# Turning queries and keys by DMA instead of on TensorE, in an attention and FFT-gate kernel

## The chip, the cores and the metric

The kernel runs on one core of a Trainium2 chip. The metric is the device time of one execution in microseconds (us), less is better. Most executions of one kernel agree within some tenths of a per cent; a run that is more than 1.5% above the fastest of its kernel is called slow and is left out of the ratios.

## The reference

Four batches of local and global attention feed a gated convolution. Cut to what matters:

```python
# attention: q, k, v are (4 batches, 8 heads, 768 rows, 64)
scores = scale * np.matmul(q, k.transpose(0, 1, 3, 2))
is_global = pos[None, :] < 8                   # the first 8 keys are seen by all queries
is_local = (rel >= 0) & (rel < 96)             # and each query sees its last 96 keys
...                                            # slope bias, mask, softmax
attn = np.matmul(a, v)
# gate
proj = x @ w_proj                              # 512 -> 3 x 512
y = x1 * irfft(rfft(x2) * rfft(filter)) * x3
out = y @ w_out
```

The kernel's score matmuls read queries and keys with the head dimension on the partitions, so both are needed turned (`QT`, `KT`), while they are loaded row by row (`qn`, `kn`). The kernel works on 7 key tiles a batch. A tile has 128 places: the first 8 are for the global keys, the other 120 are for rows of the sequence. So each key tile needs the 8 global key columns in front of its own.

## The kernel before

The kernel is written as a list of operations. Each one names its engine, an expected duration, and keys for what it reads and writes. A list scheduler lays these on the engines' time lines, with a table of small tuned numbers ("nudges") that shift its choices. The program is then emitted in one order, and semaphores are derived from overlapping addresses in that emitted order.

```python
    def load_rows(self, what, dst, src, b, t):           # places 8.. of a tile; 0 to 7 stay
        lo, hi = self.K0[t], self.K0[t] + KL
        self.load("G", dst[P - (hi - lo):P, t, :, 0:self.D], ...)

    def transposes(self, what, t, src, cols):
        b = g.bank()
        def turn(_):
            for i in range(4):
                nc.tensor.transpose(b.f16()[:, P * i:P * i + P],
                                    src[:, 2 * i:2 * i + 2, :], self.ident)
        g.op("P", pe(*[128] * 4), turn, acq=[b], r=["ident", (what + "n", t)] + ..., name=what)
        lo = NG if what == "k" else 0                    # NG = 8: leaves the global columns out
        dst = self.QT[:, :, cols:cols + P] if what == "q" else self.KT[:, :, cols + lo:cols + P]
        g.op("AV", ..., lambda e: self.copy(e, dst, b.f16()...[:, :, lo:]), use=[b],
            w=[(what.upper() + "T", t)], name=what + "T")
        if what == "k" and t == 0:                       # global columns of all 7 tiles
            kv = self.KT.rearrange("p i (t c) -> p i t c", t=7)
            g.op("V", dve(224), lambda _: self.copy(
                "V", kv[:, :, :, 0:NG], kv[:, :, 0:1, NG:2 * NG].to_broadcast([P, 4, 7, NG])),
                r=[("KT", 0)], w=["KTg"])

    def attention(self, b):
        for c in range(3):                               # thirds of a batch
            for t in ([0, 1, 2], [3, 4], [5])[c]:
                self.transposes("q", t, self.qn[:, t], P * t)
            for t in self.GRP[c]:
                self.transposes("k", t, self.kn[:, t], P * t)
            for i in range(4):
                self.scores(i, c, ...)                   # read ("QT", t), ("KT", t) and "KTg"
            ...                                          # values, projection, gate

    def program(out):                                    # the order of emission
        for o in out:
            need[o] = set(o.preds)                       # from keys and PSUM banks alone
            ...
        while len(order) < len(out):
            for e in "AVSGP":                            # first engine whose next op is ready
                if line[e] and need[line[e][-1]] <= done:
                    ...
                    break
```

"A", "V", "S", "G" and "P" are ScalarE, VectorE, SyncE (a DMA queue), GpSimd and TensorE. The small copy (`"KTg"`) reads tile 0's first turned rows and writes 8 columns of every key tile.

## Time and profile before

| | before |
|---|---|
| time, median of 3 runs | 176.94 us (176.42 to 177.24) |
| TensorE busy, of a 175.5 us span | 166.9 us, 95% |
| VectorE, ScalarE busy | 157.0 us, 152.6 us |
| TensorE transposes of `qn`, `kn` tiles | 156 matmuls |
| hardware DMA queue | 4,424 packets, 7.30 MB |

The prediction below reads the page of this kernel. Here are three of its lines that it does not show: the busy tenths of TensorE and VectorE and the granted TensorE clock, in 40 slices of 4.4 us (9 is 90% or more).

```profile
PE   7799999999899799999999999999999999999991
DVE  6669778999999769999999998999899999998960
PEclk9999999999999999999999999999999999999998
```

### The profile page before, as it was taken

To read this page: it belongs to the slowest core of one execution; us is meant where nothing else is said; L and a number is where in the kernel's file an instruction comes from. 1 tells how busy PE (TensorE), PEld (TensorE's weight loads), DVE (VectorE), ACT (ScalarE), POOL (GpSimd) and SP (SyncE) were. 2 spreads that over 40 slices of the span, in tenths; PEclk is the share of its full clock that TensorE was granted. 3 is DMA by queue.
4 is the path that set the end of the run, shared out by engine and by line. 5 is a ranking of instruction groups with operands and counts; after the bars stand their busy time and mean duration, and the time that the engine had idled before them with its cause. 6 is when DMAs were issued, how large, how long until landed. Compare 5 with 4: busy or idle time off the path is not lost.

```text
span 175.5 us, 4566 instructions
## 1 busy us (share of the span) xinstructions
PE 166.9 (95%) x1768; PEld 104.3 (59%) x1768; DVE 157.0 (89%) x368; ACT 152.6 (87%) x304; POOL 75.3 (43%) x97
## 2 busy tenths in 40 slices
PE   7799999999899799999999999999999999999991
PEld 2357777665457567575446669754556674547540
DVE  6669778999999769999999998999899999998960
ACT  8879989999999778999997977999799897968751
POOL 7999986298997699998040300000000000000000
PEclk9999999999999999999999999999999999999998
DMA  5999999999999999999999900000710000043145
GB/s 177 148 145 134 146 200 209 166 152 138 135 166 159 132 141 142 146 144 149 66 63 344 70 4 4 0 0 0 294 70 4 0 2 4 0 159 140 60 166 197
DMA packets 79853, 20.06 MB, mean 114 GB/s; under 512 B 70528, under 2 KB 76888, under 8 KB 79832
## 3 DMA queue, kind: packets, MB, share of 16 engines
q0 software_dynamic: 75408, 12.47, 107.2%
q1 hardware_dynamic: 4424, 7.30, 11.5%
q8 instruction: 14, 0.23, 0.5%
q14 instruction: 7, 0.06, 0.1%
HBM read 25.69 MB, written 6.29 MB: 182 GB/s over the span
## 4 chain that ended last, share of the span: by engine, by line
PE 64%; DVE 14%; DMA 9%; POOL 5%; ACT 5%; issue 2%; ACTq 0%; POOLq 0%; DVEq 0%
PE bank L1098 19%; PE bank L1215 12%; DMA qn<-in_q_dram 9%; PE bank L1159 6%; PE bank L1181 4%; PE bank L1015 4%; PE bank L924 4%; PE bank L938 3%; PE bank L1020 3%; PE bank L975 3%; PE bank L1060 3%; ACT E L990 3%; POOL kn L583 2%; POOL vn L583 2%; PE bank L630 2%
## 5 line engine op out<-in xcount | busy, mean ns | idle before, releaser
L1098 PE MATMUL bank<-xT,w 128*128 128x384 f16 x256 | 45.6, 326 | 0.0
L990 ACT ACTIVATE E<-bank 128x864 f16<-128x864 f32 x48 | 41.0, 923 | 1.7 <-PE bank L975 1.3
L1098 PEld LDWEIGHTS <-w 128*128 128x128 f16 x256 | 23.9, 98 | 15.8 <-issue 0.8
L583 POOL DMA_DIRECT2D kn<-in_k_dram x24 | 21.6, 908 | 14.0 <-PE bank L938 6.6
L583 POOL DMA_DIRECT2D vn<-in_v_dram x29 | 26.2, 922 | 2.0 <-DMA w<-in_moe_w_proj_dram 1.6
L1215 PE MATMUL bank<-wo,y 128*128 128x512 f16 (+1 forms) x100 | 21.8, 371 | 0.1
L583 POOL DMA_DIRECT2D qn<-in_q_dram x21 | 18.6, 892 | 5.9 <-PE bank L755 3.2
L997 DVE TENSOR_TENSOR E<-E,mask 128x864 f16<-128x864 f16 x36 | 20.9, 597 | 0.1
L1039 DVE TENSOR_TENSOR xn<-bank,rc 128x512 f16<-128x512 f32 (+1 forms) x24 | 18.5, 775 | 0.4
L571 ACT ACTIVATE ot<-bank 128x512 f32<-128x512 f32 (+1 forms) x23 | 13.1, 606 | 5.1 <-PE bank L1215 5.0
L1108 ACT CAST g<-bank 128x384 f16<-128x384 f32 x32 | 15.7, 494 | 1.4 <-PE bank L1098 1.2
L1015 PEld LDWEIGHTS <-E 128*128 128x128 f16 x224 | 14.1, 97 | 3.6 <-DVE E L997 1.1
L571 ACT ACTIVATE ab<-bank 128x512 f16<-128x512 f32 x23 | 14.3, 633 | 2.2 <-PE bank L1159 2.0
L1215 PEld LDWEIGHTS <-y 128*128 128x128 f16 x100 | 9.5, 98 | 10.7 <-DVE y L1257 0.8
L1015 PE MATMUL bank<-vn,E 128*128 128x65 f16 x224 | 15.8, 194 | 0.0
L571 ACT ACTIVATE x<-bank 128x384 f16<-128x384 f32 x28 | 13.8, 507 | 2.3 <-PE bank L1098 1.8
L1020 PE MATMUL bank<-vn,E 128*128 128x65 f16 x192 | 15.4, 193 | 0.0
L975 PE MATMUL bank<-QT,KT 64*128 64x216 f16 (+2 forms) x224 | 15.0, 241 | 0.1
L1020 PEld LDWEIGHTS <-E 128*128 128x128 f16 x192 | 13.3, 97 | 0.4
L567 ACT CAST X<-bank 128x512 f16<-128x512 f32 x21 | 12.3, 643 | 0.0
L975 PEld LDWEIGHTS <-KT 64*128 64x128 f16 x224 | 8.3, 94 | 5.6 <-issue 3.0
L924 PE MATMUL bank<-ab,fwd 128*128 128x512 f16 x40 | 11.4, 379 | 0.0
(144 smaller groups left out, 358.2 us busy)
## 6 DMA issues: line engine op xcount, KB each, us to landing
out_dram<-ot SPq DMA_DIRECT2D x23, 256.0 KB
vn<-in_v_dram POOLq DMA_DIRECT2D x28, 120.0 KB, 6.1
kn<-in_k_dram POOLq DMA_DIRECT2D x21, 120.0 KB, 6.0
qn<-in_q_dram POOLq DMA_DIRECT2D x18, 128.0 KB, 6.7
w<-in_moe_w_proj_dram POOLq DMA_DIRECT2D x4, 256.0 KB, 7.3
g<-in_moe_filter_fft_dram POOLq DMA_DIRECT2D x1, 768.0 KB, 12.5
qn<-in_q_dram POOLq DMA_DIRECT2D x3, 192.0 KB, 5.0
kn<-in_k_dram POOLq DMA_DIRECT2D x3, 192.0 KB, 5.1
```

What stands on the lines that cost most here:

```text
L571: self.nc.scalar.mul(out, in_, c)
L583: return self.g.op(eng, 0.57 + 0.00035 * nbytes[0] if eng == "G" else 0.5, lambda _: e.dma_start(dst, src), w=w, r=r, nbytes=nbytes, name= ...
L924: self.nc.tensor.matmul(b.f32(), self.fwd[:, f], src(i, t), start=(n == 0), stop=(n == len(terms) - 1))
L975: nc.tensor.matmul(bs[hh].f32()[:, off:off + w], self.KT[hs, hp, P * m:P * m + P], self.QT[hs, hp, KL * m:KL * m + w], start=(off == 0 and ...
L990: g.op("A", act(864), lambda _: nc.scalar.activation(eo, bs[0].two()[:, :, 0:432].rearrange("p h (m w) -> p h m w", m=2), Act.Exp, scale=s ...
L997: g.op("V", dve(864, 2), lambda _: nc.vector.tensor_mul(eo, eo, mk), r=[("E", hp, gi), ("mask", hp)], w=[("E", hp, gi)], name="masked")
L1015: nc.tensor.matmul(o[:, n, hh], ef[:, at:at + P], vt[:, t, 2 * hp + hh, :], start=first, stop=(t == 0), skip_group_check=True)
L1020: nc.tensor.matmul(o[:, n, hh], ef[:, at:at + P], vt[:, t - 1, 2 * hp + hh, :], start=False, stop=True, skip_group_check=True)
L1039: nc.vector.tensor_mul(to, o[:, :, :, 0:D], rc.to_broadcast([P, 2, 2 * nt, D]))
L1098: nc.tensor.matmul(bk.f32()[:, 0:h], self.w[:, c, o + P * j:o + P * j + P], self.xT[:, c, h * s:h * s + h], start=(c == 0), stop=(c == 3))
L1108: g.op("A", act(h), lambda _: nc.scalar.copy(x3, pts[1].f32()[:, 0:h]), use=[pts[1]], w=[ko], name="x3")
L1215: nc.tensor.matmul(bk.f32()[:, 0:n], y[:, c, P * t:P * t + P], self.wo[:, c, cs], start=(c == 0), stop=(c == 3))
```

## The change

Its intent: 18 of the tiles (all 13 of batch 3; queries 4 and 5 and keys 4 to 6 of batch 2) are turned by the transposing DMA, straight from `qn`/`kn` into `QT`/`KT`. That takes 72 transposes off TensorE and 18 copies off ScalarE and VectorE. The schedule allows 1.9 us of SyncE for each. In batch 3, where even key tile 0 goes that way, two small DMAs put the global rows in front of each `kn` tile, so the transposition itself delivers the global columns, and the small copy falls away. In batch 2 tile 0 is still turned on TensorE, and the small copy stays. The rest of the diff is a new order, a few more idle matmuls (matmuls on dummy data that fill waits of TensorE) and a new expected size of one load in the schedule. All nudges are replaced (cut here).

```diff
-    FAVOUR = 0.1
+    FAVOUR = 0.0
...
-                gap = o.start - at - 2.2 * (at < BEGIN + 1.0)
+                gap = o.start - at - 1.7 * (at < BEGIN + 1.0)
...
+    CROSS = frozenset((b, w, t) for b in (2, 3) for w in "qk" for t in range(7) if b > 2 or t > 3)
...
+    def turned(self, b, what, t, src, cols):
+        if (b, what, t) not in self.CROSS:
+            self.transposes(what, t, src, cols)
+            return
+        dst = (self.QT if what == "q" else self.KT)[:, :, cols:cols + P]
+        keys = [("kng", min(t // 2, 1))] if what == "k" else []
+        self.g.op("S", 1.9, lambda _: self.nc.sync.dma_start_transpose(
+            out=dst, in_=src.rearrange("p h d -> p (h d)")), r=[(what + "n", t)] + keys,
+            w=[(what.upper() + "T", t)], nbytes=(512, 1000), name=what + "T")
+        if what == "k" and t == 0:
+            self.g.writer["KTg"] = self.g.writer[("KT", 0)]
...
-                    self.transposes("q", t, self.qn[:, t], P * t)
+                    self.turned(b, "q", t, self.qn[:, t], P * t)
...
-                    self.transposes("k", t, self.kn[:, t], P * t)
+                    self.turned(b, "k", t, self.kn[:, t], P * t)
...
+                if t == 0 and (b, "k", 0) in self.CROSS:
+                    self.load_global(self.kn, ("kng",), ("kn", 0))
```

## The prediction

> **What bounds the kernel now.** I read the page first, for the share of each engine and for the chain of work that ended last.
>
> ```profile
> PE 166.9 (95%) x1768; PEld 104.3 (59%) x1768; DVE 157.0 (89%) x368; ACT 152.6 (87%) x304; POOL 75.3 (43%) x97
> ...
> PE 64%; DVE 14%; DMA 9%; POOL 5%; ACT 5%; issue 2%; ACTq 0%; POOLq 0%; DVEq 0%
> ```
>
> TensorE is the fullest engine and holds most of the chain, but VectorE and ScalarE are close behind, so an average does not say what a saving on TensorE is worth. Next I asked for the busy time by stage. The columns are start and end, length, then busy time and instructions of PE, PEld, DVE, ACT, POOL, then the granted clock, the DMA share and GB/s.
>
> ```profile
> 0.00:58.00 58.00, 54.03 (x684) 34.43 (x684) 50.08 (x142) 53.55 (x115) 48.28 (x67) 1.00 2.05 159
> 58.00:88.00 30.00, 29.20 (x293) 18.29 (x294) 27.33 (x59) 27.04 (x52) 23.60 (x27) 1.00 2.17 130
> 88.00:102.00 14.00, 13.95 (x142) 8.44 (x142) 13.81 (x29) 12.79 (x25) 3.44 (x4) 1.00 0.88 150
> 102.00:171.00 69.00, 69.00 (x647) 42.74 (x645) 65.32 (x141) 58.37 (x115) 0.00 (x0) 1.00 0.15 57
> 171.00:175.50 4.50, 0.72 (x7) 0.39 (x4) 0.42 (x1) 0.80 (x2) 0.00 (x0) 0.84 0.54 201
> ```
>
> From 88 to 171 us TensorE has no hole at all. A busy PE may still be stalled in small ways, so I counted the columns that its matmuls stream in each stage and divided by 2,400 columns a microsecond (53 ns for 128 columns, against 55 ns from start to start in the chain; two row or column tiles that run together count once). That gives 26.6 us of pure streaming in the 30 us from 58 to 88, but about 81.5 in the 83 us from 88 to 171. So the last 83 us are set by the amount of TensorE work; before that, waits for DMA (one of 9.4 us in the chain, from 49 to 58 us) and VectorE (nearly every piece of the chain from 66 to 88 us) count too.
>
> Then I looked for the transposes that the change removes in the chain in order of time (start, length, what):
>
> ```profile
> 107.22 0.45 PE bank L938 x8
> ...
> 109.61 1.12 PE bank L938 x20
> 110.73 0.34 PE bank L1060 x6
> 111.06 0.89 PE bank L938 x16
> ```
>
> L938 is the TensorE transpose of queries and keys. Batch 3's stand in the chain itself, 4 matmuls in 0.22 us.
>
> **What the Trainium skill says.** "VectorE: DVE Perf Modes", section "The three transpose paths", gives 390 ns for a 128x128 transpose on TensorE and 1309 ns by the DMA crossbar. The trace agrees for TensorE only in kind: one is 219 ns long here, and pipelined ones cost 55 ns each. "Advanced Engine Details and Errata", section "X-Bar Transpose (TRN2)", says that transposing DMAs are as fast as ordinary ones, and "DMA: Bandwidth & Descriptors", section "Latency and other measured facts", has 261 GB/s measured for one kernel. No run here shows either yet. The latter page, section "Issuing engines are not separate DMA queues", says that all queues share the same 16 engines; the trace has both queues at work, and while loads run the engines are full.
>
> **The change, part by part.** A tile is 128 rows of 512 fp16 numbers. The set has 5 tiles of batch 2 (queries 4 and 5, keys 4 to 6) and all 13 of batch 3: 18.
>
> Removed: 18 x 4 = 72 TensorE transposes and 18 copies out of PSUM.
>
> ```profile
> L938 PE MATMUL bank<-ident,kn x84: 216/219/219, 38.1 to 111.7; 128*128 128x128 f16 x84
> ...
> L567 ACT COPY KT<-bank 128x480 f16<-128x480 f16 x15 | 8.8, 604 | 0.6 <-PE bank L938 0.6
> L567 ACT COPY QT<-bank 128x512 f16<-128x512 f16 x13 | 8.0, 626 | 0.5 <-PE bank L938 0.5
> ...
> L567 DVE COPY QT<-bank 128x512 f16<-128x512 f16 x5 | 2.1, 418 | 0.9 <-PE bank L938 0.9
> ```
>
> On TensorE that is 72 x 55 ns = 4.0 us. By their order 17 of the 18 tiles are turned between 87 and 112 us, in the full stretch, so 3.7 us are on the path. The copies: the instruction order of the changed kernel has 10 fewer KT and 6 fewer QT copies of this size on ScalarE (10 x 0.604 + 6 x 0.626 = 9.8 us) and 2 fewer on VectorE (0.8 us). The scheduler then shifts other work to ScalarE: 4 eo copies, one group of xn scalings, and others back. Summing the counts that differ by the durations of these rows, VectorE has some 5 us less and ScalarE some 6 us less. So all three engines lose 3 to 4% together and none becomes the new bound.
>
> Added: 18 transposing DMAs and 2 small ones (the global rows of keys for batch 3) on the SP queue, which until now issues 35 DMAs and waits most of the time:
>
> ```profile
> SPq L1221 <- ACT ot L571: 81.7, 18, 28.5
> ```
>
> At 261 GB/s a tile of 128 KB is 0.5 us of transfer (an estimate, from the skill); the schedule takes 1.9 us of SP and some 1.5 us of DMA for each. At 2 us a tile, 18 are 36 us of the SP queue. Batch 3's queries and keys leave GpSimd from 68 to 98 us and its scores begin at 117 us, so 13 x 2 = 26 us fit between. The DMA engines:
>
> ```profile
> DMA  5999999999999999999999900000710000043145
> GB/s 177 148 145 134 146 200 209 166 152 138 135 166 159 132 141 142 146 144 149 66 63 344 70 4 4 0 0 0 294 70 4 0 2 4 0 159 140 60 166 197
> ```
>
> Each slice is 4.4 us. They are full until slice 23 (101 us) and then nearly idle. The five tiles of batch 2 and the first of batch 3 compete with loads, the rest does not. I put a delay of the loads at up to 2 us, at a place where they are 10 to 20 us ahead.
>
> Moved: the whole order is laid anew (new nudges, and FAVOUR 0 in place of 0.1, so VectorE is not avoided). 25 idle matmuls in place of 16: 14 in front instead of 11, four in a hole before the first values, the rest in small holes. The front ones fill the 1.02 us that PE waits at 6.1 us for the first queries; they remove no wait, and the clock is already 1.00 there, so I give them 0 (plus or minus 0.3).
>
> Sum: -3.7 in the full stretch; -0.3 to -1 for the relieved VectorE before 88 us; +0.3 to +1.5 for what a new order and dependence on DMA landings cost. Net about -3.7, so 176.94 becomes 173.2.
>
> **Rivals.** A: the crossbar is slow. At 1309 ns for each 128x128 block (the skill), a tile is 5.2 us and 18 are 94 us, not before about 160 us for the last. Scores of batch 3 would wait, and the time would be 185 or more. For it: the only figure for this very operation. Against: the same skill's "as fast as regular DMAs", and a schedule with 2 us, which looks measured. At 3 us a tile, batch 3's last third would come some microseconds late: 175 to 178.
>
> B: the SP queue becomes the wait. It takes its DMAs in order, and the stores of batch 1 now stand between transposes that wait for loads. There are six output buffers; a late store holds ScalarE's copy, then a bank, then TensorE. The new order shows such waits on DMA at several ot copies. It would eat 1 to 3 us: 174 to 176.
>
> C: the saving is given back in the first half. If loads and VectorE set when batch 2 and 3 can begin, less TensorE work only makes holes before 112 us. Against it: the streaming count of 81.5 in 83 us. It would leave 175 to 176.
>
> D: a better packing of the first 88 us, where about 7 us of stall lie between 40 and 88, would give 171.
>
> **Range and chances.** The saving by count puts the time at 173.2, just past the 2% line (173.4). D, at 0.2, pulls below 172; B and C, together 0.3, pull to 174 to 176; A in a mild form, 0.07, goes above 176.5, seldom far. Range 170.9 to 176.3. Faster 0.52, same 0.42, slower 0.06.
>
> **What would show each step.** L938 must have 84 matmuls instead of 156, PE busy less by about 4 us net of 9 more idle matmuls (2 us); KT and QT copies of this size on ScalarE, 16.8 us before, must be about 7. From about 88 us to the last matmul TensorE must still be full, and the stretch shorter by 3 to 4 us; if it has holes that end with a DMA into QT or KT, A is true, and the SP queue's timeline will show more than 2 us a tile. Holes that end with ScalarE's ot, itself after a DMA to the output, mean B. A stretch that starts later than 88 us by as much as it is shorter means C. One thing besides time: for batch 2 nothing loads rows 0 to 7 of the key tiles that the crossbar turns, and it writes these rows over the global key columns, so a small numerical error is possible. The prediction is wrong if time falls although PE's last stretch does not shrink, or if DMA landings enter the chain after 88 us.

## More of the kernel before

TensorE is nearly full throughout, and its granted clock is at 9 tenths or more in all but the last slice. The stage from 60 to 80 us (columns: start and end, length, busy time and instructions of PE, PEld, DVE, ACT, POOL, granted clock, DMA share, GB/s) and, in VectorE's timeline (start, length, what), the copy of batch 2's global columns:

```profile
60.00:80.00 20.00, 19.84 (x212) 13.20 (x210) 18.25 (x39) 18.27 (x39) 20.00 (x23) 1.00 2.25 141
```

```profile
61.88 0.26 DVE L567 COPY KT<-KT 128x224 f16<-128x224 f16 x1
```

That copy costs a quarter of a microsecond and stands behind no wait. It is 4 x 7 x 8 = 224 elements a partition: the 8 columns of all seven tiles.

## The result, and the profile after

The change made the kernel slower: 186.68 us median of 4 runs (184.29 to 188.91), against 177.01 us (176.42 to 177.24) for the kernel before. Two of the four runs count as slow; the fast ones are 184.29 and 185.78. The ratio of fast runs is 1.0459, 95% interval 1.0375 to 1.0543. Here and below a ratio is the mean time of one kernel's fast runs over that of the other's fast runs of the same rounds, so it is not quite the ratio of the medians quoted. The result of the changed kernel is correct.

The profile below is of a run of 187.57 us, one of the slow ones. What is read from it does not depend on that: an experiment below (one tile moved) has the same wait at the same place in a fast run.

First the page: busy time, and the share of each engine in the chain that ended last.

```profile
PE 166.1 (89%) x1705; PEld 102.3 (55%) x1705; DVE 149.6 (80%) x359; ACT 149.3 (80%) x301; POOL 75.2 (40%) x97
...
PE 62%; DMA 15%; POOL 8%; DVE 7%; ACT 2%; issue 2%; SPq 1%; POOLq 0%; DVEq 0%; ACTq 0%
```

Work has fallen on every compute engine, VectorE by 7.4 us, TensorE by only 0.8. So more work on them is not the cause. DMA's share of the chain rose from 9% to 15%. The slices (4.6 us each) show where:

```profile
PE   7995999999999960079999999999999999999992
...
DVE  6635669999998820089999998979999999999960
...
PEclk9999699999999996559999999999999999999999
```

TensorE and VectorE both have one long hole, from 66 or 68 to 79 us, and the clock falls there. (It also falls at 19 to 23 us in this slow run; the fast profiles of e1 and e5 do not have that dip, so nothing is read from it.) In the two stages around the hole TensorE is busy 8.07 of 20 us, then 19.89, and the clock is 0.77, then 0.89:

```profile
60.00:80.00 20.00, 8.07 (x116) 5.57 (x115) 6.05 (x14) 8.41 (x16) 11.20 (x13) 0.77 2.36 133
80.00:100.00 20.00, 19.89 (x155) 11.89 (x155) 19.46 (x44) 16.91 (x33) 17.15 (x19) 0.89 1.90 119
```

Who waited for whom is in the list of waits (engine and line, what ended the wait; us in all, times, longest):

```profile
DVE KT L564 <- DMA KT<-kn: 13.3, 1, 13.3
...
PE bank L934 <- DVE xT L564: 11.9, 1, 11.9
ACT QT L564 <- PE bank L934: 11.8, 1, 11.8
POOL qn L580 <- PE bank L934: 9.6, 1, 9.6
```

Read from the top, it is a row of dominoes: each line waits for the one above it. VectorE waits for a DMA, TensorE for VectorE, ScalarE and GpSimd for TensorE. Only the first is a cause. VectorE's timeline there:

```profile
65.30 0.68 DVE L570 TENSOR_SCALAR h<-bank 128x512 f16<-128x512 f32 x1
79.30 0.22 DVE L564 COPY KT<-KT 128x224 f16<-128x224 f16 x1 [13.32 <-DMA KT<-kn]
79.44 0.45 DVE L564 COPY xT<-bank 128x576 f16<-128x576 f16 x1
```

It is the small copy of the global columns, the one that ran at 61.88 us without a wait before. It now waits 13.3 us for the transposing DMA of `kn` into `KT`. Behind it stands the copy of `xT`, which frees the PSUM bank for which TensorE waits. The chain in order of time shows what the DMA did:

```profile
65.84 6.32 DMA kn<-in_k_dram
...
74.85 4.33 DMA KT<-kn
...
79.30 0.22 DVE KT L564
```

The load of a later key tile lands at 72.2 us. Then SyncE issues three transposes, one after another, and the last lands at 79.2 us. In the built program their order is tile 5, tile 6, tile 4 (columns 640, 768 and 512 of `KT`); that matters for e5 below. So a copy that needs tile 0 alone waits until tiles 4, 5 and 6 have been loaded and turned.

Why it waits is in the instruction lists of the two programs, which give the semaphores that each VectorE instruction waits for:

```
before  147 L567 TensorCopy KT<-KT 128x28x8  [waits DVE_49,PE_49]
after   150 L564 TensorCopy KT<-KT 128x28x8  [waits DMAHW3_49,DMAHW4_49,DMAHW2_49,DVE_49]
```

Three DMA semaphores stand there, one for each of keys 4 to 6 of batch 2. The TensorE path wrote a key tile from column 8 on (`lo = NG`). The transposing DMA writes all 128 columns, the 8 global ones included. The keys of the schedule do not know this: `("KT", 4)` and `"KTg"` are different names. In the emitted order the three DMAs come ahead of the copy, so the step that works by addresses has to make the copy wait for them. It is right to do so: the copy has to overwrite what the DMA put there.

### The profile page after: what moved, and what is told of

The parts are those of the page before. It is cut to its first block, busy times and chain, and to the rows that moved or that the text cites. A ratio compares the mean times of both kernels' runs of the same rounds, so it can differ in the third digit from the quotient of the medians.

```text
span 185.8 us, 4477 instructions
## 1 busy us (share of the span) xinstructions
PE 166.1 (89%) x1705; PEld 102.3 (55%) x1705; DVE 149.6 (80%) x359; ACT 149.3 (80%) x301; POOL 75.2 (40%) x97
## 3 DMA queue, kind: packets, MB, share of 16 engines
q1 hardware_dynamic: 14288, 9.72, 21.1%
## 4 chain that ended last, share of the span: by engine, by line
PE 62%; DMA 15%; POOL 8%; DVE 7%; ACT 2%; issue 2%; SPq 1%; POOLq 0%; DVEq 0%; ACTq 0%
PE bank L1106 19%; PE bank L1223 11%; PE bank L1167 10%; DMA qn<-in_q_dram 5%; PE bank L1189 5%; DMA vn<-in_v_dram 4%; PE bank L983 4%; PE bank L920 4%; DMA kn<-in_k_dram 3%; POOL kn L580 2%; DMA KT<-kn 2%; POOL qn L580 2%; PE bank L1068 2%; PE bank L1023 2%; PE bank L1028 2%
## 5 line engine op out<-in xcount | busy, mean ns | idle before, releaser
L1106 PE MATMUL bank<-xT,w 128*128 128x384 f16 x256 | 46.5, 332 | 0.1
L998 ACT ACTIVATE E<-bank 128x864 f16<-128x864 f32 x48 | 41.5, 921 | 2.9 <-PE bank L983 2.7
L1106 PEld LDWEIGHTS <-w 128*128 128x128 f16 x256 | 24.6, 99 | 17.0 <-issue 2.3
L1223 PE MATMUL bank<-wo,y 128*128 128x512 f16 (+1 forms) x100 | 22.5, 371 | 0.0
L568 ACT ACTIVATE ot<-bank 128x512 f32<-128x512 f32 (+1 forms) x25 | 14.8, 634 | 4.1 <-PE bank L1223 3.8
L1047 DVE TENSOR_TENSOR xn<-bank,rc 128x512 f16<-128x512 f32 (+1 forms) x23 | 17.7, 774 | 0.2
L568 ACT ACTIVATE ab<-bank 128x512 f16<-128x512 f32 x23 | 13.8, 637 | 3.1 <-PE bank L1167 3.1
L564 ACT COPY QT<-bank 128x512 f16<-128x512 f16 (+1 forms) x9 | 5.8, 642 | 11.9 <-PE bank L934 11.8
L934 PE MATMUL bank<-ident,qn 128*128 128x128 f16 x40 | 4.1, 228 | 11.9 <-DVE xT L564 11.9
L1028 PEld LDWEIGHTS <-E 128*128 128x128 f16 x192 | 13.3, 97 | 1.2 <-issue 0.3
L564 ACT CAST eo<-bank 128x384 f16<-128x384 f32 x29 | 12.2, 503 | 0.9 <-DVE rc L1052 0.6
```

What stands on the lines that cost most here:

```text
L564: {"A": nc.scalar.copy, "V": nc.vector.tensor_copy, "G": nc.gpsimd.tensor_copy}[e](out, in_)
L568: self.nc.scalar.mul(out, in_, c)
L998: g.op("A", act(864), lambda _: nc.scalar.activation(eo, bs[0].two()[:, :, 0:432].rearrange("p h (m w) -> p h m w", m=2), Act.Exp, scale=s ...
L1028: nc.tensor.matmul(o[:, n, hh], ef[:, at:at + P], vt[:, t - 1, 2 * hp + hh, :], start=False, stop=True, skip_group_check=True)
L1047: nc.vector.tensor_mul(to, o[:, :, :, 0:D], rc.to_broadcast([P, 2, 2 * nt, D]))
L1106: nc.tensor.matmul(bk.f32()[:, 0:h], self.w[:, c, o + P * j:o + P * j + P], self.xT[:, c, h * s:h * s + h], start=(c == 0), stop=(c == 3))
```

## The experiments

The theory: this one wait is the whole loss, the crossbar work itself is hidden, and the saving on TensorE is there as predicted. The first rival: the new order is worse by itself. The second: 18 transposing DMAs are too slow, or hold up loads. The third: the saving on TensorE is worth nothing. Each edit is against the changed kernel unless it says otherwise. e1, e2, e3 and e0 ran in one call, e8, e5, e6, e7 in a second, and e9, e10, e11 in a third; the kernel before had fast means of 176.53, 176.50 and 176.57 us in these. All results were correct within the tolerance.

| experiment | median us | ratio to before (95%) | wait of a global-column copy for DMA |
|---|---|---|---|
| changed kernel | 186.68 | 1.0459 (1.0375 to 1.0543) | 13.3 us |
| e1, copy emitted first | 172.41 | 0.9784 (0.9737 to 0.9831) | none |
| e2, rows loaded, copy of four tiles | 173.33 | 0.9815 (0.9768 to 0.9862) | none |
| e3, batch 3 only | 182.72 | 1.0341 (1.0289 to 1.0394) | none |
| e0, no crossbar | 190.73 | 1.0795 (1.0742 to 1.0849) | none |
| e8, two copies | 175.44 | 0.9926 (0.9879 to 0.9972) | 2.5 us |
| e5, one tile back in the first copy | 185.60 | 1.0519 (1.0464 to 1.0574) | 13.8 us |
| e6, e8 and 72 transposes | 180.80 | 1.0243 (1.0189 to 1.0297) | 3.2 us |
| e7, e8 and idle matmuls as before | 174.57 | 0.9862 (0.9807 to 0.9916) | 1.3 us (profile of a slow run) |
| e9, e8, second copy later | 172.83 | 0.9794 (0.9759 to 0.9830) | none |
| e10, e9 and idle matmuls as before | 171.94 | 0.9747 (0.9707 to 0.9788) | none |
| e11, e9 and every transpose twice | 183.63 | 1.0360 (1.0298 to 1.0423) | 1.0 us |

### e1: the wait turned around, nothing else

The three transposes of batch 2's keys are emitted after the copy, so they wait for it instead. The order of instructions on every engine is the same as in the changed kernel, so this separates the theory from the first two rivals. The global columns of tiles 4 to 6 then hold what the DMA read from rows 0 to 7 of `kn`, which nothing loads in this batch, so this version is a probe and not a right kernel (the error stayed within the tolerance).

```diff
-            need[o] = set(o.preds)
+            need[o] = set(o.preds) | LATE.get(o, set())
...
-        self.g.op("S", 1.9, lambda _: self.nc.sync.dma_start_transpose(
+        o = self.g.op("S", 1.9, lambda _: self.nc.sync.dma_start_transpose(
...
+        if what == "k" and b == 2:
+            LATE[o] = {self.g.writer["KTg"]}
```

> One wait is turned round and nothing else: VectorE's copy of the global key columns of batch 2 is put ahead of the three crossbar transposes of keys 4 to 6 in the program, so that the copy no longer waits for them (all instruction orders are the same as in the changed kernel; the global columns of tiles 4 to 6 then hold stale rows, a small numerical error is accepted). Theory W (that wait is the loss): the 13.3 us wait of the copy for the DMA into KT goes to under 1 us, TensorE's hole of 11.9 us at 68 us goes, the granted clock of that stage returns to about 1.0, and 186.7 becomes 173 to 175.5, under the kernel before. Rival X (the crossbar or its contention with loads is slow): the hole only moves to the scores of batch 2 or 3 and the time stays over 180. Rival O (the new order is bad in itself): the hole goes but the time stays at 178 to 181.

Measured: 172.41 us, ratio 0.9784, a little under the range expected. VectorE's timeline, and the stage that had the hole:

```profile
65.47 0.55 DVE L567 COPY KT<-KT 128x224 f16<-128x224 f16 x1
```

```profile
60.00:80.00 20.00, 19.89 (x215) 13.61 (x214) 18.97 (x42) 18.61 (x39) 16.61 (x19) 1.00 2.65 123
```

The copy runs at 65.5 us without a wait, TensorE is busy 19.89 of 20 us, and the clock is 1.00. The difference of the two ratios is 0.0675, at 176.5 us 11.9 us, as much as the 11.9 us that TensorE waited for VectorE (the intervals leave some 1.7 us either way, so the match to a tenth is luck). The order and the 18 transposes are unchanged (the instruction lists of the two built programs are the same on every engine, but for waits), so the first two rivals cannot explain the loss.

### e2: the right data in another way

The copy writes tiles 0 to 3 only; for tiles 4 to 6 one small DMA puts the global rows into `kn` ahead of the transposes, as the change does for batch 3. The overlap is gone and the data is right.

```diff
+        self.kn[0:NG, 4:7] <- self.kn[NG:2 * NG, 0:1] broadcast to 3 tiles   # one SyncE DMA
...
-                "V", kv[:, :, :, 0:NG], kv[:, :, 0:1, NG:2 * NG].to_broadcast([P, 4, 7, NG])),
+                "V", kv[:, :, 0:n, 0:NG], kv[:, :, 0:1, NG:2 * NG].to_broadcast([P, 4, n, NG])),  # n = 4
```

(The first line is shortened; it is a DMA placed in the laid order ahead of the transposes, which wait for it.)

> The same wait removed in a way that keeps the result right: the global rows of key tiles 4 to 6 of batch 2 are put into the key buffer by one more small DMA before the crossbar turns them, and VectorE's copy writes only tiles 0 to 3, so the two no longer write the same columns. Instruction orders as in the changed kernel, but for that DMA. Theory W: within 1% of the first run (173 to 175.5), and an error against the reference as small as that of the kernel before. Rival X: over 180, and 2 us worse than the first run for the added DMA ahead of three transposes.

Measured: 173.33 us, ratio 0.9815, within the interval of e1. No wait of VectorE for the crossbar is left. A new one appears on GpSimd, which is 44% busy; with it e2 is still within 0.4% of e1:

```profile
POOL kn L592 <- DMA kn<-kn: 5.5, 1, 5.5
```

Two removals of the overlap by different means agree, which speaks for the theory. (How large the error was stays unchecked.)

### e3 and e0: fewer crossbar tiles, or none, in the new order

These were to show the new order by itself: the changed kernel with only batch 3 turned by DMA, and with none.

```diff
-    CROSS = frozenset((b, w, t) for b in (2, 3) for w in "qk" for t in range(7) if b > 2 or t > 3)
+    FULL = frozenset((b, w, t) for b in (2, 3) for w in "qk" for t in range(7) if b > 2 or t > 3)
+    CROSS = frozenset(x for x in FULL if x[0] == 3)        # e3;  e0: "if False"
```

The nudges of all other operations are kept.

> The crossbar for batch 3 alone; the five tiles of batch 2 go back to TensorE (the nudges of all other operations kept, the scheduler lays the order anew). Theory W: there is no crossbar transpose that the global copy of batch 2 could wait for, so no hole; 13 of 18 tiles saved, 2.9 of 4.0 us: 174 to 177. Rival X: the 13 tiles of batch 3 are the greater part of the crossbar's work, so most of the loss stays: over 181. Rival O: 179 to 182.

> No crossbar at all: all 18 tiles on TensorE, with the new nudges, FAVOUR 0 and the idle matmuls of the changed kernel. Theory W: the loss goes with the crossbar; the kernel is near the one before, 176 to 180 (the nudges were found for another set of operations). Rival O (the new order is the loss): 183 or more.

Measured: 182.72 us (ratio 1.0341) and 190.73 us (1.0795). Both are misses: e3 lies in the range written down for the crossbar as the cause (over 181), e0 in that for the new order (183 or more). The wait on the crossbar is gone, as it should be, but the scheduler laid everything anew for the other set of operations, and other waits came, first e3's, then e0's:

```profile
DVE mix L1249 <- ACT eo L570: 4.5, 1, 4.5
```

```profile
DVE g L1125 <- ACT g L1123: 7.8, 3, 6.4
```

A likely reason is that the nudges were tuned for one set of operations. Since both runs have other orders than the changed kernel, they cannot say what its order costs or brings; what speaks against the two rivals is e1, which keeps that order and all 18 transposes and is faster than the kernel before. The later experiments therefore hold the laid order and change single instructions in it.

### e8 and e5: the dose

In e8 the first copy writes tiles 0 to 3, so it overlaps no transpose. A second small VectorE copy writes the global columns of tiles 4 to 6 from tile 3, put in at the place where the schedule expects the transposes to have landed. e5 is the same with one tile (4) back in the first copy, so the copy waits for one transpose, not three. It was meant as a smaller dose of the wait.

```diff
-                "V", kv[:, :, :, 0:NG], kv[:, :, 0:1, NG:2 * NG].to_broadcast([P, 4, 7, NG])),
+                "V", kv[:, :, 0:n, 0:NG], kv[:, :, 0:1, NG:2 * NG].to_broadcast([P, 4, n, NG])),
...                                                         # n = 4 in e8, 5 in e5
+            d.fn = lambda _: self.copy("V", kv[:, :, 4:7, 0:NG], kv[:, :, 3:4, 0:NG].to_broadcast([P, 4, 3, NG]))
...                                                         # 5:7 and 2 tiles in e5
+        at = max(o.landed for o in preds if o.bytes)       # after the landings, by the schedule
+        i = next(i for i, o in enumerate(out) if o.eng == "V" and o.start > at)
+        out.insert(i, d)
```

> The wait removed without a further DMA and with a right result: VectorE's copy of the global columns writes tiles 0 to 3 at its old place, and a second copy writes tiles 4 to 6 after the crossbar transposes have landed in the schedule, ahead of the scores that read them. All orders as in the changed kernel but for that one small copy. Theory W: 172 to 174, as the first run (172.41); the second copy waits for the DMA for less than 1 us. If the second copy comes too early on VectorE, it holds it for 1 to 3 us and the time is 174 to 176.

> A dose of the suspected wait: as the kernel with two copies, but the first copy writes tiles 0 to 4, so it has to wait for one of the three crossbar transposes (keys 4, the first of the three) instead of for all or none. Theory W: in the changed kernel the three were issued from 72.2 to 76.0 us and the last landed at 79.2, so the first lands some 2.5 us earlier; VectorE waits 9.5 to 11.5 us there, and the time is 7 to 11 us over the kernel with two copies: 180 to 184. Rival (only the last transposes or contention matter): under 176.

Measured: e8 175.44 us (0.9926), the second of the two outcomes expected, e5 185.60 us (1.0519), over its range. First e8's second copy in VectorE's timeline, then e5's first:

```profile
82.10 0.19 DVE L576 COPY KT<-KT 128x96 f16<-128x96 f16 x1 [2.48 <-DMA KT<-kn]
```

```profile
77.14 0.20 DVE L576 COPY KT<-KT 128x160 f16<-128x160 f16 x1 [13.80 <-DMA KT<-kn]
```

In e8 the schedule was too hopeful by 2.5 us, and the second copy waits. In e5 the wait was expected to be 9.5 to 11.5 us and came out at 13.8, because tile 4 is not the first of the three transposes, as the expectation says, but the last in SyncE's list. The chains show it, first e5's, then e8's:

```profile
70.06 1.19 SPq L975
...
71.36 1.20 SPq L975
...
72.73 4.32 DMA KT<-kn
```

```profile
73.20 8.77 DMA KT<-kn
```

So e5 is no smaller dose: its copy waits for one DMA in place of three, but for the one that lands last, and the whole loss is back. In e8 the last of the three landed 8.77 us after its issue, twice as long as in e5 and in the changed kernel (4.33). A likely reason, not tested, is that GpSimd's loads went on in e8 and stood still in the hole of the other two.

### e9: the second copy later

e8 left one wait, so e9 moves the second copy 6 us further on in the schedule (12 places on VectorE, not the six of the expectation).

```diff
-        at = max(o.landed for o in preds if o.bytes)
+        at = max(o.landed for o in preds if o.bytes) + 6.0
```

> The kernel with two copies, the second copy moved six places later on VectorE (behind it lay a wait of 2.5 us for the last transpose, with a hole in TensorE at a clock of 0.91). Theory W, time follows the wait one for one: the wait goes to 0 and the time to 172 to 173.5, right result, 2% under the kernel before. If the 3 us between the first run and the kernel with two copies came from something else: 175 again.

Measured: 172.83 us, ratio 0.9794. The copy is at 86 us and waits for nothing:

```profile
86.12 0.49 DVE L576 COPY KT<-KT 128x96 f16<-128x96 f16 x1
```

With e8 and e5 this is a series in one and the same laid order: no wait 0.9794, 2.5 us of wait 0.9926, 13.8 us 1.0519. In time that is 2.3 us for 2.5 us of wait and 12.8 us for 13.8, some 0.93 us for each us; the changed kernel itself has 11.7 us for 13.3. (Each wait is that of one profile.) The wait accounts for the loss. While the copy waits, VectorE runs none of its later instructions (nothing from 66.0 to 79.3 us in the changed kernel), and almost nothing of that is made up elsewhere.

### e6: is the saving on TensorE real?

e8 with 72 transposes put back on TensorE as dummies, six in each score group of batch 3, written to a bank that is about to be overwritten. If the prediction's view of the last stretch holds, their time must come back.

```diff
+            for x in range(6 * late):
+                nc.tensor.transpose(bs[0].f16()[:, 0:P], self.ident, self.ident)
```

> The saving by itself: to the kernel with two copies I add 72 transposes of 128 columns on TensorE again (of the identity, into a bank that the scores overwrite), 6 ahead of each of batch 3's 12 score groups, without their copies out of PSUM. If TensorE's work sets the end there, as the prediction said, they cost 72 x 55 ns = 4.0 us: 3 to 4.5 us over the kernel with two copies. Rival C (the saving falls into holes): under 1.5 us.

Measured: 180.80 us, ratio 1.0243, 5.6 us over e8 where 3 to 4.5 us were expected. About 0.7 us of it may be a longer wait of the second copy (3.2 us instead of 2.5, one profile of each). From that copy to the end e6's profile is 96.7 us long and e8's 91.5, so 5.2 us come after it. So the third rival falls: TensorE work there is paid in full, and somewhat more. What the remaining excess over the 4.0 us of streaming is, no run settles; the dummies sit ahead of the scores, and ScalarE waits 4.4 us for scores in e6 against 0.6 in e8.

### e7 and e10: the idle matmuls

e8 and e9 with the constant that sizes the idle matmuls in front put back as before. It makes 12 in front instead of 14 (the kernel before has 11), 23 in all instead of 25.

```diff
-                gap = o.start - at - 1.7 * (at < BEGIN + 1.0)
+                gap = o.start - at - 2.2 * (at < BEGIN + 1.0)
```

> The part of the change in front alone undone: the two idle matmuls that 1.7 in place of 2.2 adds are taken out of the kernel with two copies (12 in front in place of 14). The prediction gave them nothing: within 0.3 us of the kernel with two copies. If they keep the clock up for the first transposes of queries, taking them out costs 0.5 to 1.5 us and the clock of the first 20 us falls below 0.99.

> The same with 12 idle matmuls in front in place of 14, so that this part of the change is compared without a DMA wait in between: within 0.5 us of the run before it, whichever way; 1 us worse if the idle matmuls matter for the first transposes.

Measured: e7 174.57 us (0.9862), 1.1 us less than e8 by the ratios, where 0.3 was expected at most. Its second copy waits 1.3 us, which is 1.2 us less than in e8, but this is the profile of a slow run (176.92 us), so whether the gain is the shorter wait is not shown. e10 is 171.94 us (0.9747, interval 0.9707 to 0.9788), against 0.9794 for e9: 0.8 us less, where 0.5 was expected at most. In both pairs the intervals overlap. So no gain from the two extra idle matmuls is seen, and a cost of some tenths of a microsecond is likelier.

e10 is right in its data, beats both kernels, and is the one version whose gain is over 2% with its whole interval: 2.5% faster than the kernel before, 6.8% faster than the changed one by the two ratios (0.9747 / 1.0459).

### e11: the crossbar twice

e9 with every transposing DMA issued a second time into a buffer that nobody reads, to see how much room the crossbar has.

```diff
+        def twice(_):
+            self.nc.sync.dma_start_transpose(out=dst, in_=src2)
+            self.nc.sync.dma_start_transpose(out=self.spare[self.turns % 3], in_=src2)
```

> Every crossbar transpose issued twice, the second time into a spare buffer that nobody reads: twice the SP time (18 x 1.2 us more) and twice the transposes' load on the DMA engines. If the crossbar is hidden, as theory W needs, the time is within 1.5 us of the kernel with the later second copy; if the crossbar itself or its contention with loads is near the path (rivals A, B, X), 3 us or more are added, with waits of scores for DMAs into QT or KT.

Measured: 183.63 us, ratio 1.0360, 10.0 us over e9. By the expectation this is the outcome of the rivals ("3 us or more"). Now TensorE does wait for transposes:

```profile
ACT E L1031 <- PE bank L1014: 6.9, 5, 3.8
PE bank L1014 <- DMA QT<-qn: 5.7, 3, 4.0
```

At 18 transposes there is no such wait in the profiles of e1, e9 and e10, and at most 0.4 us (of weight loads) in e2; at 36 there is. So the 18 are hidden, but not by far: the wide margin that the prediction saw on this queue is not there. Whether SyncE's issue or the DMA engines set the limit at 36 was not told apart; the second reads also keep `qn` and `kn` in use for longer (SyncE waits 2.3 us for one before it writes to `kn`).

## Why the prediction was wrong

It said 173.2 us, faster or the same; it was 186.68, slower.

- **The step that failed** is the part on what the change adds, together with the sentence "So all three engines lose 3 to 4% together and none becomes the new bound." The new DMAs were examined for how long they take and whether they land before the scores of batch 3, and the waits on DMA in the new instruction order were looked at for ScalarE's `ot` copies. No one asked who else writes the bytes that a transposing DMA writes. VectorE's small copy does. In the sum it is the term "+0.3 to +1.5 for what a new order and dependence on DMA landings cost". The runs show in its place one wait of 13.3 us on VectorE, which stops TensorE for 11.9 us; e1 turns this wait alone around and the time is 172.41 us.
- **The overlap was seen and taken for another thing.** The prediction says that the crossbar "writes these rows over the global key columns, so a small numerical error is possible". Two writers of the same bytes are either a race or a wait. It was a wait: the three DMA semaphores stood in the program before it ran.
- **None of the rivals was it.** A (crossbar slow), B (queue and stores), C (saving given back) and D (packing) are all about durations or amounts. A's time, "185 or more", is what was measured, but by luck: with the wait gone, all 18 transposes are in e1 at 172.41 us. A hole that ends with a DMA into KT, A's mark, did come, but ahead of the 88 us from which it was to be looked for, and on VectorE, which waited at 66 us for DMAs of tiles that are not needed until later. The last criterion, "if DMA landings enter the chain after 88 us", looked at the wrong place for the same reason; the transposes entered at 74.9 to 79.2 us.
- **The removed work was sized about rightly.** 84 matmuls are left of the transposes, as predicted. Those `QT` and `KT` copies on ScalarE are 4.2 + 2.9 = 7.1 us in the changed kernel, predicted "about 7". In e1, at full clock, VectorE is busy 6.5 us less than before and ScalarE 3.9 us less, where 5 and 6 were predicted. With the wait gone, e1 saves 3.8 us by its ratio (0.0216 x 176.5) and e10 4.5 us, where the sum said 3.7. The chain's last stretch on TensorE runs from 90.0 to 168.0 us in e1 and from 88.8 to 171.0 before: 4.2 us shorter, as its mark asked (3 to 4), and 1.2 us later. That the net comes so near 3.7 is in part luck, since e6 pays 5.6 us for the same 72 transposes. TensorE is full in e9 from 88 to 160 us (72.00 of 72 us busy), as it was before.
- **One sum does not come out.** At the chain's own pace (20 matmuls of 512 columns in 4.32 us), with the score matmuls, which overlap (12 of 216 columns in 0.66 us), and the few on 64 columns of the array counted half, the trace gives 26.6 us for 58 to 88 us, as stated, but about 80 and not 81.5 for 88 to 171. The stretch had some 3 us of small stalls, and "full" was a little too strong; e6 shows that the conclusion holds all the same.
- **The pace of the transposes was sized within reason, their landing was not asked for.** At 2 us a tile the estimate was on the safe side for issue: SyncE holds one of the query tiles for a median of 1.21 us. The estimate of 0.5 us of transfer a tile was low: 18 more of them took 14.4 us of all 16 DMA engines in e11 (e11 less e9), 0.8 us each. And from issue to landing the last of the three key tiles took 4.33 us, in e8 8.77. That is late enough to be dear to anyone who waits for it.
- **Loads and idle matmuls.** A delay of the loads of "up to 2 us" could be seen neither way once the hole was there (GpSimd waited 9.6 us behind TensorE). The idle matmuls were given 0 within 0.3 us; with two fewer, e7 and e10 came out 1.1 and 0.8 us faster, each within the noise, so they rather cost something.
- **Left open:** what the new order is worth without the crossbar (e0 and e3 were laid anew and cannot say), what `FAVOUR` and the nudges do alone, and where e6's excess over 4.0 us comes from.

## What to carry to other kernels

When a DMA takes over work from an engine, write down every instruction that reads or writes the same bytes, and look in the new program for each that now waits for this DMA's semaphore, above all on an engine that runs nothing past a waiting instruction, as VectorE here: a schedule that knows only its own names does not show such a wait. An overlap that looks like a matter of right or wrong data can be a matter of time as well. To test one suspect in a tuned kernel, hold the laid order and change the one wait; a kernel laid anew with a part undone brings waits of its own.

## What the Trainium skill lacked or had wrong

- "Advanced Engine Details and Errata", section "X-Bar Transpose (TRN2)", says that transposing DMAs are as fast as regular ones. Here they took longer by two measures. On the queue SyncE holds a transpose of a 128x512 fp16 query tile for a median of 1.21 us, against 0.33 us for the store of an output tile of twice the bytes in the same profile. On the DMA engines, the hardware queue goes from 9.72 MB and 26.1% of 170.9 us in e9 to 12.09 MB and 32.5% of 181.7 us in e11: 14.4 us of all 16 engines for 2.37 MB of transposes (the changed kernel against the one before gives 19.0 us for 2.42 MB), against 20.2 us for 7.30 MB of ordinary DMAs in the kernel before. For each MB that is 2 to 3 times as much. The ordinary ones are mostly stores in larger packets (1,650 bytes on average, against 242) and at other times.
- "VectorE: DVE Perf Modes", section "The three transpose paths", gives 1309 ns for a 128x128 block and says nothing of several in a row. Here three tiles, 12 blocks, took 7.0 us from the first issue (72.18 us) to the last landing (79.18), where 12 times that figure is 15.7 us. So blocks overlap, and the figure times their number is too high for a row of them.
- None of the pages that I read has a warning that a transpose moved from TensorE to the crossbar loses the choice of columns that the copy out of PSUM gave, and so can overlap columns that another engine fills, with a wait as the price. Here that was 13.3 us for 8 columns a tile.
